# Decode attention on one core: K and V loaded in 2 KB runs with K four batches ahead, and the output projection turned round

## The chip, the cores and the metric

One core of one Trainium2 chip. The metric is device time in microseconds of the core, the median of several executions. A "span" is the length of the profiled execution, some 2 us shorter than the time reported for the same execution.

## The reference

One new token per sequence (32 sequences), 32 query heads on 8 K/V heads, attention over the last 512 of 2048 cached keys. Cut to what matters:

```python
B, Sq, D = 32, 1, 512
Hq, Hkv, Sk, Dh = 32, 8, 2048, 128
W = min(4096, max(256, Sk // 4))                     # 512 keys
q = (x @ wq) -> [B, Hq, 1, Dh]
k, v = k_cache[:, :, Sk - W:], v_cache[:, :, Sk - W:]  # each K/V head serves 4 query heads
p = softmax(q k^T / sqrt(Dh)); o = p v
return o -> [B, 1, Hq * Dh] @ wo
```

Everything is bf16. K and V of the window are 32 MiB each, wq and wo 4 MiB each: 75.5 MB are read for little arithmetic.

## The kernel before

Four sequences ("batches") make a block of 128 query rows; there are eight blocks. For each batch 1 MiB of K and 1 MiB of V come in, K is transposed on TensorE and evicted, and the scores of the block's 32 (batch, head) pairs accumulate in one PSUM tile through a masked q. Then come softmax, transposes of p, and PV.

```python
kpool = ... bufs=5;  vpool = ... bufs=7;  ktpool = ... bufs=6
# wo: four nc.scalar.dma_start, right after the q projection
def k_ap(b):                                          # v_ap(b) the same
    return k_cache[b, :, k0:Sk, :].rearrange("g (p c) d -> p g (c d)", c=NC)   # NC = 4: runs of 4*128*2 B = 1 KB
for j in range(NBLK):
    ...
    for bb in range(BB):
        nc.sync.dma_start(out=knat[:], in_=k_ap(b))
        nc.sync.dma_start(out=vt[:], in_=v_ap(b))
        # 32 transposes of 128x128 -> kps (PSUM); copies to kt on VectorE and ScalarE
    for bb, g:  nc.tensor.matmul(sc[:], lhsT=mask_flat[...], rhs=kt_tiles[bb][:, g, :], ...)
    # reduce_max, Exp -> p_sb, reciprocal, p_sb *= rs
    for c in range(NC):  nc.tensor.transpose(pT_ps[:, c, :], p_sb[:, c * P : (c + 1) * P], ident[:])
    nc.vector.tensor_copy(out=pT_sb[:], in_=pT_ps[:])
    for bb, g, c:  nc.tensor.matmul(oT[:, 4 columns], lhsT=v_tiles[bb][:, g, c * Dh : (c + 1) * Dh], rhs=pT_sb[...])
    # oT -> O_all
for h in range(Hq):
    nc.tensor.matmul(out_ps[:], lhsT=O_all[:, h, :], rhs=wo_sb[:, h, :], start=(h == 0), stop=(h == Hq - 1))
```

## Time and profile before

| | before |
|---|---|
| time, median before the prediction (3 runs) | 246.91 us (244.85 to 247.32) |
| span of the profiled execution | 242.8 us |
| DMA row | full from 6 to 218 us; 348 GB/s once wq is in |
| TensorE busy | 182.4 us, 75% |
| mean granted TensorE clock | 0.817 |
| last K landed at | 219.3 us |
| from there to the end | 23.5 us |

How to read it: first the rows of the page that cut the span into 40 slices, to see whether one resource is full from end to end; then the table of windows, for its rate in stages that differ; then the chain of waits in order of time, for what lies after the last load. The lines themselves are in the prediction.

### The profile page before, as it was taken

Reading aid. Unit: us, or ns where it says so; the run is one execution under the profiler, and the core shown is the slowest. Engines: PE = TensorE matmul, PEld = TensorE weight load, DVE = VectorE, ACT = ScalarE, POOL = GpSimd, SP = SyncE. Lnnn points to the kernel's source line nnn. Section 1 sums busy time; section 2 is a strip of 40 time slices with the busy share of each in tenths; the row PEclk is TensorE's granted clock in tenths of the full one; section 3 lists DMA queues with packets and bytes.
Section 4 is the critical chain, followed back from the end, with each engine's and each line's share of the span. In section 5 each row is a group of like instructions: output and inputs, shape, how many; then the busy total and the mean of one; then the engine's idle time right before and its main releaser. Section 6 shows DMA issues by size and latency. Waiting matters only on the chain.

```text
span 242.8 us, 5379 instructions
## 1 busy us (share of the span) xinstructions
PE 182.4 (75%) x2483; PEld 135.8 (56%) x2500; DVE 81.8 (34%) x146; ACT 50.0 (21%) x59; POOL 2.5 (1%) x7
## 2 busy tenths in 40 slices
PE   0327232988996869789969976899699969986694
PEld 0326232558754837486748744866496649654631
DVE  3023020235335315423553434136333453344201
ACT  0000130212132113301520422113402420232000
POOL 4000000000000000000000000000000000000000
PEclk9999675699599659965995899569956995699769
DMA  5999999999999999999999999999999999991000
GB/s 201 388 362 348 348 348 348 349 348 349 348 348 348 349 351 348 349 348 349 348 349 348 349 349 348 349 350 351 348 349 350 348 350 348 341 337 58 3 0 5
DMA packets 72950, 75.90 MB, mean 313 GB/s; under 512 B 1184, under 2 KB 70880, under 8 KB 72928
## 3 DMA queue, kind: packets, MB, share of 16 engines
q1 hardware_dynamic: 68768, 71.37, 91.6%
q10 hardware_dynamic: 4160, 4.19, 5.4%
q8 instruction: 19, 0.31, 0.5%
q14 instruction: 3, 0.02, 0.0%
HBM read 75.53 MB, written 0.03 MB: 311 GB/s over the span
## 4 chain that ended last, share of the span: by engine, by line
DMA 45%; PE 36%; SPq 8%; DVE 5%; ACT 2%; issue 2%; ACTq 0%
DMA knat<-in_k_cache_dram 36%; PE kps L158 13%; PE oT L213 11%; PE sc L175 7%; SPq L151 5%; DMA wq_t<-in_wq_dram 5%; DMA wo_sb<-in_wo_dram 5%; PE out_ps L232 4%; SPq L149 3%; ACT p_sb L190 2%; DVE mx L185 2%; PE pT_ps L204 1%; DVE p_sb L200 1%; SPq L88 1%; DVE rs L199 0%
## 5 line engine op out<-in xcount | busy, mean ns | idle before, releaser
L158 PE MATMUL kps<-ident,knat 128*128 128x128 bf16 x1024 | 79.7, 247 | 25.6 <-DMA knat<-in_k_cache_dram 23.4
L158 PEld LDWEIGHTS <-knat 128*128 128x128 bf16 x1024 | 73.6, 113 | 35.3 <-DMA knat<-in_k_cache_dram 28.3
L164 DVE COPY kt<-kps 128x1024 bf16<-128x1024 bf16 x86 | 57.5, 689 | 89.5 <-PE kps L158 89.1
L166 ACT COPY kt<-kps 128x1024 bf16<-128x1024 bf16 x42 | 42.5, 1013 | 127.0 <-PE kps L158 127.0
L175 PE MATMUL sc<-kt,maskB 128*128 128x512 bf16 x120 | 34.9, 427 | 1.1 <-issue 0.9
L175 PE MATMUL sc<-kt,maskA 128*128 128x512 bf16 x119 | 33.3, 415 | 1.0 <-issue 0.7
L213 PEld LDWEIGHTS <-vt 128*128 128x128 bf16 x1024 | 28.5, 103 | 1.0 <-issue 0.6
L213 PE MATMUL oT<-pT_sb,vt 128*128 128x4 bf16 x1024 | 28.4, 166 | 0.5 <-DVE pT_sb L206 0.5
L175 PEld LDWEIGHTS <-maskA 128*128 128x128 bf16 x128 | 13.3, 109 | 14.5 <-issue 5.1
L175 PEld LDWEIGHTS <-maskB 128*128 128x128 bf16 x128 | 13.3, 110 | 14.5 <-issue 6.0
L204 PE MATMUL pT_ps<-ident,p_sb 128*128 128x128 bf16 x32 | 3.8, 254 | 17.0 <-DVE p_sb L200 16.8
L221 DVE CAST O_all<-oT 128x128 bf16<-128x128 f32 x8 | 5.8, 719 | 26.0 <-PE oT L213 26.0
L204 PEld LDWEIGHTS <-p_sb 128*128 128x128 bf16 x32 | 2.2, 110 | 20.6 <-DVE p_sb L200 20.6
L96 PE MATMUL qT_ps<-xT_sb,wq_t 128*128 128x32 bf16 x128 | 4.1, 188 | 8.1 <-DMA wq_t<-in_wq_dram 8.1
L232 PE MATMUL out_ps<-wo_sb,O_all 128*32 128x512 bf16 x32 | 8.9, 447 | 0.8 <-DVE O_all L221 0.8
L190 ACT ACTIVATE p_sb<-sc,nbias 128x512 bf16<-128x512 f32 x8 | 5.5, 688 | 18.6 <-DVE nbias L187 18.6
L185 DVE TENSOR_REDUCE mx<-sc 128x1 f32<-128x512 f32 x8 | 5.5, 692 | 9.9 <-PE sc L175 9.9
L96 PEld LDWEIGHTS <-wq_t 128*128 128x128 bf16 x128 | 3.7, 104 | 8.5 <-DMA wq_t<-in_wq_dram 8.5
L166 ACT ACT_TABLE_LOAD x1 | 1.3, 1283 | 29.2 <-DMA knat<-in_k_cache_dram 29.2
L232 PEld LDWEIGHTS <-O_all 128*32 128x32 bf16 x32 | 3.5, 111 | 5.8 <-issue 2.4
L103 DVE CAST qT_sb<-qT_ps 128x1024 bf16<-128x1024 f32 x1 | 1.2, 1225 | 12.0 <-PE qT_ps L96 12.0
L206 DVE COPY pT_sb<-pT_ps 128x512 bf16<-128x512 bf16 x8 | 3.4, 424 | 4.1 <-PE pT_ps L204 4.1
(18 smaller groups left out, 14.9 us busy)
## 6 DMA issues: line engine op xcount, KB each, us to landing
knat<-in_k_cache_dram SPq DMA_DIRECT2D x32, 1024.0 KB, 12.0
vt<-in_v_cache_dram SPq DMA_DIRECT2D x32, 1024.0 KB, 11.9
wq_t<-in_wq_dram SPq DMA_DIRECT2D x4, 1024.0 KB, 8.5
wo_sb<-in_wo_dram ACTq DMA_DIRECT2D x4, 1024.0 KB, 19.3
x_sb<-in_x_dram SPq DMA_DIRECT2D x1, 32.0 KB, 1.6
out_dram<-out_sb SPq DMA_DIRECT2D x1, 32.0 KB, 1.5
```

The lines of the kernel that those rows point to most:

```text
L96: nc.tensor.matmul(qT_ps[:, h, :], lhsT=wq_t[:, cc, hl * Dh : (hl + 1) * Dh], rhs=xT_sb[:, cc, :], start=(cc == 0), stop=(cc == CC - 1),)
L149: nc.sync.dma_start(out=knat[:], in_=k_ap(b))
L151: nc.sync.dma_start(out=vt[:], in_=v_ap(b))
L158: nc.tensor.transpose(kps[:, gi, c, :], knat[:, g, c * Dh : (c + 1) * Dh], ident[:])
L164: nc.vector.tensor_copy(out=dst, in_=src)
L166: nc.scalar.copy(out=dst, in_=src)
L175: nc.tensor.matmul(sc[:], lhsT=mask_flat[:, P * t : P * t + P], rhs=kt_tiles[bb][:, g, :], start=(t == 0), stop=(t == NT - 1),)
L185: nc.vector.reduce_max(out=mx[:], in_=sc[:], axis=AX.X)
L190: nc.scalar.activation(out=p_sb[:], in_=sc[:], func=ACT.Exp, bias=nbias[:], scale=scale, accum_out=ssum[:],)
L204: nc.tensor.transpose(pT_ps[:, c, :], p_sb[:, c * P : (c + 1) * P], ident[:])
L213: nc.tensor.matmul(oT[:, rep * t : rep * t + rep], lhsT=v_tiles[bb][:, g, c * Dh : (c + 1) * Dh], rhs=pT_sb[:, c, rep * t : rep * t + rep] ...
L232: nc.tensor.matmul(out_ps[:], lhsT=O_all[:, h, :], rhs=wo_sb[:, h, :], start=(h == 0), stop=(h == Hq - 1),)
```

## The change

Its intent: longer runs for the transfers that bound the kernel, nothing left to do after the last load but a little PV, and a shorter projection.

* Two K/V heads share a tile: each head gives 64 rows of 8 keys (2 KB runs), one head to the even partitions, the other to the odd ones. The scores read each head's keys with a step of two elements. p is written twice over (each key for both heads of a pair), transposed in eight pieces, and masked so that each query head keeps its own partitions; PV then takes a pair of heads at once, eight columns for four.
* The scores of a batch stand directly behind its transposes. K is issued four batches (one block) ahead of V; wo comes in four pieces during blocks 2 to 5 from SyncE.
* The projection holds wo still and streams O: 128 matmuls of 32 columns for 32 of 512, then four transposes.

```diff
+    KLEAD = BB
+    kpool = ... bufs=7      # was 5;  vpool 7 as before;  ktpool bufs=3, was 6
+        return k_cache[b, :, k0:Sk, :].rearrange("(gp g2) (p c) d -> g2 p gp (c d)", g2=2, c=2 * NC)
+        for g2 in range(2):
+            nc.sync.dma_start(out=knat[g2::2, :, :], in_=k_ap(b)[g2])      # V the same
+    for bpre in range(min(KLEAD, B)):
+        issue_k(bpre)
...
+            if b + KLEAD < B:
+                issue_k(b + KLEAD)
+            issue_v(b)
+            if bb == 0 and 2 <= j < 2 + N_WO_CHUNKS:
+                issue_wo(j - 2)
...
-                    rhs=kt_tiles[bb][:, g, :],
+                    rhs=kt[:, g // 2, :].rearrange("p (k g2) -> p g2 k", g2=2)[:, g % 2, :],
...
-        nc.vector.tensor_scalar_mul(out=p_sb[:], in0=p_sb[:], scalar1=rs[:])
+        nc.vector.tensor_scalar_mul(
+            out=p_d[:], in0=p_sb[:].unsqueeze(2).to_broadcast([P, NC * P, 2]), scalar1=rs[:]
+        )
...                                       # eight transposes of p_d for four of p_sb
-        nc.vector.tensor_copy(out=pT_sb[:], in_=pT_ps[:])
+        nc.vector.tensor_tensor(out=pT_sb[:], in0=pT_ps[:], in1=own[:] (broadcast), op=mult)
...
-                        rhs=pT_sb[:, c, rep * t : rep * t + rep],
+                        rhs=pT_sb[:, c, 2 * rep * t : 2 * rep * (t + 1)],
...
-            out_ps[:], lhsT=O_all[:, h, :], rhs=wo_sb[:, h, :],
+                outT_ps[:, mc, :], lhsT=wo_sb[:, h, mc * P : (mc + 1) * P], rhs=O_all[:, h, :],
```

More of the change, by code (lines that the diff above doesn't have):

```diff
@@ L48 @@
     M = wo.shape[1]
-    assert M <= 512
+    assert M % P == 0 and M <= 512
+    MC = M // P
+    KLEAD = BB
     x2 = x.rearrange("b q d -> (b q) d")
@@ L58 @@
     x_sb = consts.tile([B, D], BF16, name="x_sb")
-    nc.sync.dma_start(out=x_sb[:], in_=x2[:, :])
     qT_sb = consts.tile([P, Hq, B], BF16, name="qT_sb")
@@ L68 @@
     masks = [maskA, maskB]
+    par = consts.tile([P, 2], FP32, name="par")
+    nc.vector.reduce_sum(out=par[:], in_=ident[:].rearrange("q (p g) -> q g p", g=2), axis=AX.X)
+    own = consts.tile([P, P], BF16, name="own")
+    nc.vector.tensor_copy(
+        out=own[:].rearrange("q (a g i) -> q a g i", g=2, i=rep),
+        in_=par[:].unsqueeze(1).unsqueeze(3).to_broadcast([P, P // (2 * rep), 2, rep]),
+    )
+    kpool = ctx.enter_context(tc.tile_pool(name="kpool", bufs=7))
+    vpool = ctx.enter_context(tc.tile_pool(name="vpool", bufs=7))
@@ L70 @@
+    ktpool = ctx.enter_context(tc.tile_pool(name="ktpool", bufs=3))
     N_WQ_CHUNKS = 4
     WQ_CHUNK_H = Hq // N_WQ_CHUNKS
-    with tc.tile_pool(name="psq", bufs=1, space=bass.MemoryType.PSUM) as psq, tc.tile_pool(
-        name="wqp", bufs=N_WQ_CHUNKS, side="right"
-    ) as wqp:
-        xT_ps = psq.tile([P, CC, B], BF16, name="xT_ps")
-        for cc in range(CC):
-            nc.tensor.transpose(
-                xT_ps[:, cc, :], x_sb[:, cc * P : (cc + 1) * P], ident[0:B, 0:B]
-            )
-        nc.vector.tensor_copy(out=xT_sb[:], in_=xT_ps[:])
-        qT_ps = psq.tile([P, Hq, B], FP32, name="qT_ps")
-        wq_r = wq.rearrange("(cc c) n -> c cc n", c=P)
-        wq_tiles = []
-        for ci in range(N_WQ_CHUNKS):
-            h0 = ci * WQ_CHUNK_H
-            wq_t = wqp.tile([P, CC, WQ_CHUNK_H * Dh], BF16, name="wq_t")
-            nc.sync.dma_start(out=wq_t[:], in_=wq_r[:, :, h0 * Dh : (h0 + WQ_CHUNK_H) * Dh])
-            wq_tiles.append(wq_t)
-        for ci in range(N_WQ_CHUNKS):
-            h0 = ci * WQ_CHUNK_H
-            wq_t = wq_tiles[ci]
-            for hl in range(WQ_CHUNK_H):
-                h = h0 + hl
-                for cc in range(CC):
-                    nc.tensor.matmul(
-                        qT_ps[:, h, :],
-                        lhsT=wq_t[:, cc, hl * Dh : (hl + 1) * Dh],
-                        rhs=xT_sb[:, cc, :],
-                        start=(cc == 0),
-                        stop=(cc == CC - 1),
-                    )
-        nc.vector.tensor_copy(out=qT_sb[:], in_=qT_ps[:])
@@ L105, with k_ap, v_ap @@
-    kpool = ctx.enter_context(tc.tile_pool(name="kpool", bufs=5))
-    vpool = ctx.enter_context(tc.tile_pool(name="vpool", bufs=7))
-    ktpool = ctx.enter_context(tc.tile_pool(name="ktpool", bufs=6))
+    wq_r = wq.rearrange("(cc c) n -> c cc n", c=P)
+    def k_ap(b):
+        return k_cache[b, :, k0:Sk, :].rearrange("(gp g2) (p c) d -> g2 p gp (c d)", g2=2, c=2 * NC)
+    def v_ap(b):
+        return v_cache[b, :, k0:Sk, :].rearrange("(gp g2) (p c) d -> g2 p gp (c d)", g2=2, c=2 * NC)
+    knat_tiles = {}
@@ new lines, with issue_k, issue_v @@
+    v_tiles = {}
+    def issue_k(b):
+        knat = kpool.tile([P, Hkv // 2, 2 * NC * Dh], BF16, name="knat")
+        for g2 in range(2):
+            nc.sync.dma_start(out=knat[g2::2, :, :], in_=k_ap(b)[g2])
+        knat_tiles[b] = knat
+    def issue_v(b):
+        vt = vpool.tile([P, Hkv // 2, 2 * NC * Dh], BF16, name="vt")
+        for g2 in range(2):
+            nc.sync.dma_start(out=vt[g2::2, :, :], in_=v_ap(b)[g2])
+        v_tiles[b] = vt
+    nc.sync.dma_start(out=x_sb[:], in_=x2[:, :])
@@ new lines @@
+    pctx = ExitStack()
+    psq = pctx.enter_context(tc.tile_pool(name="psq", bufs=1, space=bass.MemoryType.PSUM))
+    wqp = pctx.enter_context(tc.tile_pool(name="wqp", bufs=N_WQ_CHUNKS, side="right"))
+    wq_tiles = []
+    for ci in range(N_WQ_CHUNKS):
+        h0 = ci * WQ_CHUNK_H
+        wq_t = wqp.tile([P, CC, WQ_CHUNK_H * Dh], BF16, name="wq_t")
+        nc.sync.dma_start(out=wq_t[:], in_=wq_r[:, :, h0 * Dh : (h0 + WQ_CHUNK_H) * Dh])
+        wq_tiles.append(wq_t)
+    for bpre in range(min(KLEAD, B)):
+        issue_k(bpre)
@@ new lines @@
+    xT_ps = psq.tile([P, CC, B], BF16, name="xT_ps")
+    for cc in range(CC):
+        nc.tensor.transpose(xT_ps[:, cc, :], x_sb[:, cc * P : (cc + 1) * P], ident[0:B, 0:B])
+    nc.vector.tensor_copy(out=xT_sb[:], in_=xT_ps[:])
+    qT_ps = psq.tile([P, Hq, B], FP32, name="qT_ps")
+    for ci in range(N_WQ_CHUNKS):
+        h0 = ci * WQ_CHUNK_H
+        wq_t = wq_tiles[ci]
+        for hl in range(WQ_CHUNK_H):
+            h = h0 + hl
+            for cc in range(CC):
+                nc.tensor.matmul(
+                    qT_ps[:, h, :],
+                    lhsT=wq_t[:, cc, hl * Dh : (hl + 1) * Dh],
+                    rhs=xT_sb[:, cc, :],
+                    start=(cc == 0),
+                    stop=(cc == CC - 1),
+                )
@@ L108 @@
+    nc.vector.tensor_copy(out=qT_sb[:], in_=qT_ps[:])
+    pctx.close()
     wop = ctx.enter_context(tc.tile_pool(name="wop", bufs=1, side="right"))
@@ L112, with issue_wo @@
     hw_ = Hq // N_WO_CHUNKS
-    for i in range(N_WO_CHUNKS):
-        nc.scalar.dma_start(
+    def issue_wo(i):
+        nc.sync.dma_start(
             out=wo_sb[:, i * hw_ : (i + 1) * hw_, :],
@@ L125 @@
     ops_pool = mctx.enter_context(tc.tile_pool(name="ops", bufs=1, space=bass.MemoryType.PSUM))
-    def k_ap(b):
-        return k_cache[b, :, k0:Sk, :].rearrange("g (p c) d -> p g (c d)", c=NC)
-    def v_ap(b):
-        return v_cache[b, :, k0:Sk, :].rearrange("g (p c) d -> p g (c d)", c=NC)
     kt_evac_ctr = 0
@@ L142 @@
         )
-        kt_tiles = []
-        v_tiles = []
+        sc = scps_pool.tile([P, NC * P], FP32, name="sc")
+        t = 0
         for bb in range(BB):
             b = j * BB + bb
-            knat = kpool.tile([P, Hkv, NC * Dh], BF16, name="knat")
-            nc.sync.dma_start(out=knat[:], in_=k_ap(b))
-            vt = vpool.tile([P, Hkv, NC * Dh], BF16, name="vt")
-            nc.sync.dma_start(out=vt[:], in_=v_ap(b))
-            kt = ktpool.tile([P, Hkv, NC * P], BF16, name="kt")
-            for gp in range(Hkv // 2):
-                kps = ktps_pool.tile([P, 2, NC, P], BF16, name="kps")
-                for gi in range(2):
-                    g = gp * 2 + gi
-                    for c in range(NC):
-                        nc.tensor.transpose(
-                            kps[:, gi, c, :], knat[:, g, c * Dh : (c + 1) * Dh], ident[:]
-                        )
-                dst = kt[:, gp * 2 : gp * 2 + 2, :]
-                src = kps[:].rearrange("p a c q -> p a (c q)")
+            if b + KLEAD < B:
[3 more added lines that the diff above has]
+                issue_wo(j - 2)
+            knat = knat_tiles.pop(b)
+            kt = ktpool.tile([P, Hkv // 2, 2 * NC * P], BF16, name="kt")
+            for gp in range(Hkv // 2):
+                kps = ktps_pool.tile([P, 2 * NC, P], BF16, name="kps")
+                for c in range(2 * NC):
+                    nc.tensor.transpose(kps[:, c, :], knat[:, gp, c * Dh : (c + 1) * Dh], ident[:])
+                dst = kt[:, gp, :]
+                src = kps[:].rearrange("p c q -> p (c q)")
                 if kt_evac_ctr % 3 != 2:
@@ L167 @@
                 kt_evac_ctr += 1
-            kt_tiles.append(kt)
-            v_tiles.append(vt)
-        sc = scps_pool.tile([P, NC * P], FP32, name="sc")
-        t = 0
-        for bb in range(BB):
             for g in range(Hkv):
@@ L199 @@
         nc.vector.reciprocal(out=rs[:], in_=ssum[:])
-        nc.vector.tensor_scalar_mul(out=p_sb[:], in0=p_sb[:], scalar1=rs[:])
-        pT_ps = ptps_pool.tile([P, NC, P], BF16, name="pT_ps")
-        for c in range(NC):
-            nc.tensor.transpose(pT_ps[:, c, :], p_sb[:, c * P : (c + 1) * P], ident[:])
-        pT_sb = ppool.tile([P, NC, P], BF16, name="pT_sb")
-        nc.vector.tensor_copy(out=pT_sb[:], in_=pT_ps[:])
+        p_d = ppool.tile([P, NC * P, 2], BF16, name="p_d")
+        nc.vector.tensor_scalar_mul(
+            out=p_d[:], in0=p_sb[:].unsqueeze(2).to_broadcast([P, NC * P, 2]), scalar1=rs[:]
+        )
+        pT_ps = ptps_pool.tile([P, 2 * NC, P], BF16, name="pT_ps")
+        for c in range(2 * NC):
+            nc.tensor.transpose(
+                pT_ps[:, c, :], p_d[:, c * (P // 2) : (c + 1) * (P // 2), :].rearrange("r p g -> r (p g)"), ident[:]
+            )
+        pT_sb = ppool.tile([P, 2 * NC, P], BF16, name="pT_sb")
+        nc.vector.tensor_tensor(
+            out=pT_sb[:], in0=pT_ps[:], in1=own[:].unsqueeze(1).to_broadcast([P, 2 * NC, P]), op=mybir.AluOpType.mult
+        )
         oT = ops_pool.tile([P, P], FP32, name="oT")
@@ L210 @@
         for bb in range(BB):
-            for g in range(Hkv):
-                for c in range(NC):
+            vt = v_tiles.pop(j * BB + bb)
+            for gp in range(Hkv // 2):
+                for c in range(2 * NC):
                     nc.tensor.matmul(
-                        oT[:, rep * t : rep * t + rep],
-                        lhsT=v_tiles[bb][:, g, c * Dh : (c + 1) * Dh],
-                        rhs=pT_sb[:, c, rep * t : rep * t + rep],
+                        oT[:, 2 * rep * t : 2 * rep * (t + 1)],
+                        lhsT=vt[:, gp, c * Dh : (c + 1) * Dh],
+                        rhs=pT_sb[:, c, 2 * rep * t : 2 * rep * (t + 1)],
                         start=(c == 0),
-                        stop=(c == NC - 1),
+                        stop=(c == 2 * NC - 1),
                     )
@@ L229 @@
     ops2 = ctx.enter_context(tc.tile_pool(name="ops2", bufs=1, space=bass.MemoryType.PSUM))
-    out_ps = ops2.tile([B, M], FP32, name="out_ps")
-    for h in range(Hq):
-        nc.tensor.matmul(
-            out_ps[:],
-            lhsT=O_all[:, h, :],
-            rhs=wo_sb[:, h, :],
-            start=(h == 0),
-            stop=(h == Hq - 1),
-        )
+    outT_ps = ops2.tile([P, MC, B], FP32, name="outT_ps")
+    for mc in range(MC):
+        for h in range(Hq):
+            nc.tensor.matmul(
+                outT_ps[:, mc, :],
+                lhsT=wo_sb[:, h, mc * P : (mc + 1) * P],
+                rhs=O_all[:, h, :],
+                start=(h == 0),
+                stop=(h == Hq - 1),
+            )
+    outT_sb = outp.tile([P, MC, B], BF16, name="outT_sb")
+    nc.vector.tensor_copy(out=outT_sb[:], in_=outT_ps[:])
+    out_tps = ops2.tile([B, M], BF16, name="out_tps")
+    for mc in range(MC):
+        nc.tensor.transpose(out_tps[:, mc * P : (mc + 1) * P], outT_sb[:, mc, :], ident[:])
     out_sb = outp.tile([B, M], BF16, name="out_sb")
-    nc.vector.tensor_copy(out=out_sb[:], in_=out_ps[:])
+    nc.vector.tensor_copy(out=out_sb[:], in_=out_tps[:])
     nc.sync.dma_start(out=out2[:, :], in_=out_sb[:])
```

## The prediction

> **What bounds the kernel now.** I read the page's slices first, because they show whether one resource is full from end to end.
>
> ```profile
> PE   0327232988996869789969976899699969986694
> PEclk9999675699599659965995899569956995699769
> DMA  5999999999999999999999999999999999991000
> GB/s 201 388 362 348 348 348 348 349 348 349 348 348 348 349 351 348 349 348 349 348 349 348 349 349 348 349 350 351 348 349 350 348 350 348 341 337 58 3 0 5
> DMA packets 72950, 75.90 MB, mean 313 GB/s; under 512 B 1184, under 2 KB 70880, under 8 KB 72928
> ```
>
> The DMA row is full from slice 1 to slice 35 and the rate is flat at 348 GB/s: for nine tenths of the span the transfers set the pace, and TensorE (PE row) has gaps. Nearly every packet is under 2 KB; K, V and wo come as runs of 512 elements, 1 KB. Only slices 1 and 2 are faster. Those carry wq, whose runs are 1024 elements, 2 KB. So next I read the table of windows, short ones in the wq stage and a long one in the steady stage (last three columns: granted clock, DMA share, GB/s).
>
> ```profile
> 10.00:11.00 1.00, 0.16 (x6) 0.05 (x2) 0.00 (x0) 0.00 (x0) 0.00 (x0) 1.00 1.05 389
> 11.00:12.00 1.00, 0.17 (x6) 0.17 (x7) 0.00 (x0) 0.00 (x0) 0.00 (x0) 1.00 1.05 389
> 125.00:155.00 30.00, 22.72 (x343) 17.70 (x343) 11.78 (x24) 7.52 (x10) 0.00 (x0) 0.84 1.10 348
> ```
>
> 2 KB packets run at about 389 GB/s, 1 KB packets at 348. Then the chain that ended last, in order of time: one block's boundary in the middle, and the end.
>
> ```profile
> 98.40 1.79 PE kps L158 x32
> 100.19 1.74 PE sc L175 x8
> 101.93 0.02 issue
> 101.95 0.69 DVE mx L185
> ...
> 104.33 0.40 PE pT_ps L204 x4
> 104.73 1.04 PE kps L158 x10
> 105.77 3.39 PE oT L213 x128
> ...
> 206.30 13.01 DMA knat<-in_k_cache_dram
> ...
> 219.35 1.96 PE kps L158 x32
> 221.31 1.74 PE sc L175 x8
> ...
> 226.32 3.49 PE oT L213 x128
> ```
>
> The reader sees two things. The last K lands at 219.3, and only then come its transposes, its scores, the softmax chain, all of the last block's PV, the output projection and the store: 23.5 us of the 242.8 lie after the last load. And per batch TensorE needs 1.79 + 1.74 us at full clock, far less than the 6.0 us that 2 MiB take at 348 GB/s.
>
> **What the Trainium skill says.** (1) "SBUF — State Buffer", section "Door 1: The DMA port swizzle": DMA bandwidth depends on how many of 16 SBUF ports the partitions of a transfer reach; partitions 0 to 63 reach only 8 of them and were measured at 196 GB/s against 328 for all 128. The new loads take 64 partitions, but every second one, and by the page's table those touch all 16 ports. The same section says that strided reads stay at full speed with at least two hits per 16-byte line; the new scores read keys with a step of 4 bytes, four hits. No load of the kernel before writes every second partition and no matmul of it reads with a step, so the trace neither agrees nor disagrees. (2) "DMA: Bandwidth & Descriptors", section "Why a DMA increments its semaphore by 16 and not by 1": the largest divisor up to 16 of the slowest dimension gives the number of DMA engines, so 64 rows still use 16. Which rows go to which engine it does not say for 64 rows; that is my largest doubt. (3) "VectorE: DVE Perf Modes", section "The perf-mode tier table": tensor_tensor with a PSUM operand runs at the 1x rate, a copy from PSUM at up to 2x. The trace agrees for copies: 1024 bf16 elements from PSUM took 689 ns, 1024 f32 ones 1225. (4) "TensorE: Matmul & The Clock Gate", section "HAM oscillation": an idle gap of about 3.4 us halves the clock. Here the clock falls to 0.50 after each softmax gap although that is only some 2.5 us.
>
> ```profile
> 126.00:127.50 1.50, 0.00 (x0) 0.00 (x0) 0.65 (x4) 0.78 (x2) 0.00 (x0) 1.00 1.10 348
> 129.00:130.50 1.50, 1.50 (x48) 1.50 (x45) 0.69 (x1) 0.00 (x0) 0.00 (x0) 0.50 1.10 348
> 130.50:132.00 1.50, 1.50 (x63) 1.50 (x60) 0.00 (x0) 0.00 (x0) 0.00 (x0) 0.50 1.10 347
> ```
>
> **The change part by part.** *Loads.* K and V come in 2 KB runs, 64 half-tile issues of 0.5 MiB for K and as many for V, in place of 1 KB runs. If they reach wq's rate, 1 MiB takes 1.0486/0.387 = 2.71 us, which is also the spacing at which the four wq pieces released TensorE (9.12, 11.83, 14.55). It was 1.0486/0.348 = 3.01. For 64 MiB of K and V that is 19 us less; wo keeps 1 KB runs. Total: wq done at 14.6, then 68 pieces (32 K, 32 V, 4 wo) at 2.71: loads end at 14.6 + 184 = 199 us, plus about 1 for wo, in place of 219.
>
> *Order.* K runs four batches ahead, so the last four pieces are V. After the last load only that V's share of PV would remain, not 23.5 us of chain, provided that TensorE has kept up. Counting pieces in issue order: block j's last V is piece 8j + 12 plus the wo pieces before it: block 5 at 14.6 + 56 x 2.71 = 166, block 6 at 188, block 7 at 199.
>
> *TensorE per block.* Transposes and scores 4 x (1.79 + 1.74) = 14.1 us; PV 3.4 (same 128 matmuls, each 26.5 ns, 8 columns for 4); p transposes 8 for 4, so 0.8. The softmax gap (101.93 to 104.33, 2.4 us) grows: the doubled, normalised p has 1024 elements with a step of 0 inside, so I take the 1x duration of 1024 elements, 1.2 us, for the 0.35 of now: gap 3.3. The mask multiply takes 0.7 to 1.2 for 0.42, half hidden by hoisted transposes: 0.7. Sum 22.3 us at full clock. The clock's fall to half covers some 6.8 us per block; PV in it kept its 3.4 us, the other half of it loses some 2 us: 24.3. Against that the loads' period is 8 x 2.71 = 21.7, or 24.4 in blocks 2 to 5, which carry a wo piece each. So TensorE, now well under the loads, comes level with them. Up to block 5 the loads still lead (166); after it I let TensorE set the end.
>
> *Projection.* 128 matmuls of 32 columns at PV's 26.5 ns are 3.4 us for 8.92; the extra copy (0.3), four transposes (0.3) and a final copy (0.5 for 0.68) take back about 0.4. All of this is on the path: net 5 us less.
>
> *Sum.* PV of block 5 starts at 166 to 167; two TensorE periods of 22.3 to 24.3 bring PV of block 7 to 211 to 215; PV 3.4, O_all 0.7, projection and copies 4.5, store and end 2.6 (as now, 240.2 to 242.8): span 222 to 227. The run lies 2 to 4 us above the span now (244.6 and the median 246.9 against 242.8). So about 226 us. Doubling the DVE work in the softmax costs nothing else: DVE was 34% busy.
>
> **The rivals.** *A: the half-partition loads collide.* If an engine gets four neighbouring rows, it writes to two ports in turn and shares both with another engine; in step, half the ports are idle at any time. For it: the page's 196 GB/s for 64 partitions; against it: even and odd partitions reach all ports, and nothing forces the engines into step. An estimate from the page's 27.2 GB/s per port: half overlapped gives about 280 GB/s, so 71.3 MB take 255 us and the time is 280; mild overlap at 340 gives loads to 224 and about 237 us, still faster since the tail is shorter. *B: TensorE binds throughout* because the strided score read is slower. If a score took twice its 216 ns, a block costs 6.9 us more, the period is about 30 us, and the time some 265. Against it: four hits per line. *C: TensorE is never the bound*, since transposes of the next block, whose K has landed long before, get hoisted into the softmax gap (ten already are, behind the p transposes). Then the end follows the loads more closely: PV of block 6 at 188, up to 7 us of block 7 done before it, time about 215. *D: the loads are faster but nothing else is*, because the buffers hold them back: seven V tiles are freed only by PV. Piece 20 (V of batch 7) needs PV of block 0, whose last V is piece 12: a slack of seven pieces, 19 us, so I count little on it.
>
> **Range and chances.** The main path gives 225 to 230, C 215, mild A 237, strong A or B 260 to 280. I weigh main path and C together at 0.6, mild A at 0.2, strong A or B at 0.2. That gives 226 with a range of 212 to 256; faster 0.76, same 0.07, slower 0.17. The margin for "same" (242 to 252) is thin, as the outcomes lie on either side of it.
>
> **What would show it right or wrong.** Right: GB/s in the steady slices near 385; the median spacing of landings 2.7 us per MiB; scores at full clock still 216 ns apart; PV still 3.4 us per block; no K wait of TensorE after block 1; a last stretch in which the DMA row is empty and TensorE works on. Wrong: GB/s under 340 with a full DMA row (A); scores 430 ns apart at clock 1.00 (B); the last PV waiting for V (C); gaps in the DMA row with SyncE waiting for PV (D).

## The result and the profile after

The changed kernel took 214.97 us (median of 12 runs, 214.82 to 215.28), the kernel before 245.54 us (15 runs, 244.68 to 247.32). The ratio is 0.8744 (95%: 0.8720 to 0.8767), so 12.6% faster. Ratios are computed as the mean time of one kernel's runs over that of the other's runs of the same rounds, so they are not quite the ratio of the medians quoted. Executions over 1.5% slower than the fastest of the same kernel are left out of the means. The prediction was 226 us with a range of 212 to 256.

The slices of the page of the changed kernel (tenths; the last but one row is the DMA rate):

```profile
PEclk9999999999999999999969969999799999979758
DMA  5999999999999999999999999999999999999500
GB/s 179 391 388 387 387 386 386 387 386 385 388 385 387 379 369 387 384 388 367 381 386 389 383 367 385 388 383 379 373 387 386 387 386 389 384 385 387 221 8 6
DMA packets 41207, 75.92 MB, mean 356 GB/s; under 512 B 2208, under 2 KB 6368, under 8 KB 41184
```

The rate is 383 to 389 GB/s wherever K and V move alone; the four dips, to 367 to 373 at the lowest, come where the four wo pieces with their 1 KB runs are issued (65.9, 90.5, 116.6 and 141.3 us). The row stays full to the end, and the granted clock, which fell in every block before, hardly falls (mean 0.944 for 0.817).

The chain that ended last, in order of time: start, length, what.

```profile
178.10 0.78 PE oT L243 x32
...
192.95 10.72 DMA vt<-in_v_cache_dram
...
203.72 1.03 PE oT L243 x32
204.74 0.02 issue
204.77 0.72 DVE O_all L251
205.49 0.04 issue
205.53 3.59 PE outT_ps L263 x128
```

The end now hangs on the last V, which is in at 203.7; one quarter of a block's PV (32 matmuls), the copy and the projection follow. TensorE is not far ahead here: it stands 0.40 us for the last V but one and 1.62 us for the last. From 203.7 to the end it is 9.6 us in place of 23.5. So the 29.5 us of span saved are 15.6 us of earlier loads (219.3 to 203.7) and 13.9 us of shorter tail.

TensorE's instructions in order of time, from one softmax to the next (in brackets the idle time before):

```profile
57.72 0.62 PE L229 MATMUL pT_ps<-ident,p_d 128*128 128x128 bf16 x8 [2.04 <-DVE p_d L224]
58.18 1.95 PE L187 MATMUL kps<-ident,knat 128*128 128x128 bf16 x32
59.97 1.97 PE L196 MATMUL sc<-kt,maskA 128*128 128x512 bf16 x7
61.78 0.94 PE L243 MATMUL oT<-pT_sb,vt 128*128 128x8 bf16 x32
...
77.94 0.62 PE L229 MATMUL pT_ps<-ident,p_d 128*128 128x128 bf16 x8 [2.04 <-DVE p_d L224]
```

PV (oT) comes in quarters of 32, one behind each batch of the *next* block's scores. In the kernel before it was a run of 128 between two blocks. Nothing in the source says so: the order was chosen when the source was compiled ("the scheduler", for short). A whole block takes 20.2 us (57.72 to 77.94); the periods before and after it are 20.0 and 20.6 us, with 0.23 us of waiting for K in the last of them. From the fourth on, periods are 23.6 to 26.1 us and contain waits for K, so the loads set them.

The last stretch in the table of windows (columns: PE, PEld, DVE, ACT, POOL busy, granted clock, DMA share, GB/s):

```profile
196.00:198.00 2.00, 0.50 (x8) 0.50 (x9) 1.19 (x3) 0.46 (x2) 0.00 (x0) 1.00 1.05 387
198.00:200.00 2.00, 1.22 (x47) 1.10 (x45) 0.69 (x1) 0.00 (x0) 0.00 (x0) 0.95 0.73 271
200.00:202.00 2.00, 1.60 (x59) 1.54 (x55) 0.00 (x0) 0.00 (x0) 0.00 (x0) 0.50 0.46 169
202.00:204.00 2.00, 0.38 (x14) 0.30 (x12) 0.00 (x0) 0.00 (x0) 0.00 (x0) 0.50 0.10 32
```

The loads do not stop at once. The full rate ends near 199, then the DMA share falls for 4 to 5 us. The records of single packets in the trace (the views do not print them) show 2 KB packets as quick as before, a median of 84 to 85 ns from 198 to 204 us for 88 ns earlier: so the rate falls because some of the engines are done before others. Why they are is not known.

### The profile page after: what moved, and what is told of

Same layout as the page of the kernel before. It is cut to its first block, busy times and chain, and to the rows that moved or that the text cites. A ratio compares the mean times of both kernels' runs of the same rounds, so it can differ in the third digit from the quotient of the medians.

```text
span 213.3 us, 5787 instructions
## 1 busy us (share of the span) xinstructions
PE 161.8 (76%) x2602; PEld 127.1 (60%) x2632; DVE 86.3 (40%) x149; ACT 50.0 (23%) x59; POOL 2.5 (1%) x7
## 4 chain that ended last, share of the span: by engine, by line
DMA 55%; PE 35%; DVE 3%; SPq 3%; issue 1%; ACT 1%
DMA knat<-in_k_cache_dram 44%; PE kps L187 15%; PE sc L196 13%; DMA vt<-in_v_cache_dram 11%; PE oT L243 3%; SPq L98 2%; PE outT_ps L263 2%; ACT p_sb L211 1%; DVE p_d L224 1%; SPq L115 1%; DVE mx L206 1%; PE pT_ps L229 1%; DVE O_all L251 0%; PE out_tps L274 0%; DVE rs L220 0%
## 5 line engine op out<-in xcount | busy, mean ns | idle before, releaser
L187 PE MATMUL kps<-ident,knat 128*128 128x128 bf16 x1024 | 68.2, 229 | 13.9 <-DMA knat<-in_k_cache_dram 13.9
L187 PEld LDWEIGHTS <-knat 128*128 128x128 bf16 x1024 | 63.5, 103 | 15.6 <-issue 14.6
L196 PE MATMUL sc<-kt,maskB 128*128 128x512 bf16 x112 | 31.4, 397 | 1.5 <-ACT kt L193 0.4
L243 PE MATMUL oT<-pT_sb,vt 128*128 128x8 bf16 x1024 | 30.2, 166 | 2.8 <-DMA vt<-in_v_cache_dram 2.0
L196 PE MATMUL sc<-kt,maskA 128*128 128x512 bf16 x114 | 31.0, 391 | 1.1 <-issue 0.2
L229 PE MATMUL pT_ps<-ident,p_d 128*128 128x128 bf16 x64 | 5.7, 241 | 16.7 <-DVE p_d L224 16.7
L229 PEld LDWEIGHTS <-p_d 128*128 128x128 bf16 x64 | 4.2, 107 | 17.5 <-DVE p_d L224 17.5
L233 DVE TENSOR_TENSOR pT_sb<-pT_ps,own 128x1024 bf16<-128x1024 bf16 x8 | 5.5, 692 | 6.5 <-PE pT_ps L229 6.5
L224 DVE TENSOR_SCALAR p_d<-p_sb,rs 128x1024 bf16<-128x1024 bf16 x8 | 6.0, 754 | 0.3
L139 DVE CAST qT_sb<-qT_ps 128x1024 bf16<-128x1024 f32 x1 | 1.2, 1225 | 11.8 <-PE qT_ps L132 11.8
L263 PE MATMUL outT_ps<-O_all,wo_sb 128*128 128x32 bf16 x128 | 3.6, 188 | 0.8 <-DVE O_all L251 0.8
```

What stands on the lines that cost most here:

```text
L187: nc.tensor.transpose(kps[:, c, :], knat[:, gp, c * Dh : (c + 1) * Dh], ident[:])
L196: nc.tensor.matmul(sc[:], lhsT=mask_flat[:, P * t : P * t + P], rhs=kt[:, g // 2, :].rearrange("p (k g2) -> p g2 k", g2=2)[:, g % 2, :], s ...
L224: nc.vector.tensor_scalar_mul(out=p_d[:], in0=p_sb[:].unsqueeze(2).to_broadcast([P, NC * P, 2]), scalar1=rs[:])
L229: nc.tensor.transpose(pT_ps[:, c, :], p_d[:, c * (P // 2) : (c + 1) * (P // 2), :].rearrange("r p g -> r (p g)"), ident[:])
L243: nc.tensor.matmul(oT[:, 2 * rep * t : 2 * rep * (t + 1)], lhsT=vt[:, gp, c * Dh : (c + 1) * Dh], rhs=pT_sb[:, c, 2 * rep * t : 2 * rep * ...
L263: nc.tensor.matmul(outT_ps[:, mc, :], lhsT=wo_sb[:, h, mc * P : (mc + 1) * P], rhs=O_all[:, h, :], start=(h == 0), stop=(h == Hq - 1),)
```

## The experiments

Twelve kernels, each timed in three rounds. All gave correct results except the eighth. The first six undo parts of the change, so that together with the changed kernel they show seven of the eight combinations of three parts: the 2 KB runs ("wide"), the lead of K, the new projection.

| kernel | wide | lead | projection | median us | ratio to before (95%) | span us |
|---|---|---|---|---|---|---|
| x1 | | | | 245.34 | 0.9983 (0.9953 to 1.0014) | 243.4 |
| x2 | | x | | 237.88 | 0.9682 (0.9652 to 0.9712) | 236.2 |
| x3 | x | | | 234.50 | 0.9530 (0.9481 to 0.9579) | 233.1 |
| x4 | x | x | | 220.47 | 0.8963 (0.8931 to 0.8995) | 218.5 |
| x5 | | x | x | 233.07 | 0.9464 (0.9416 to 0.9512) | 231.2 |
| x6 | x | | x | 230.48 | 0.9357 (0.9298 to 0.9416) | 227.7 |
| changed | x | x | x | 214.97 | 0.8744 (0.8720 to 0.8767) | 213.3 |

**x1: all three parts undone.** What is left is wo's later place on SyncE's queue, scores directly behind each batch, and the buffer counts.

```diff
-    KLEAD = BB
+    KLEAD = 0
-    ... "(gp g2) (p c) d -> g2 p gp (c d)", g2=2, c=2 * NC     (and all that goes with it)
+    ... "g (p c) d -> p g (c d)", c=NC
-    128 projection matmuls and four transposes
+    32 projection matmuls
```

> The changed kernel with its three main parts undone: 1 KB runs and the old PV, K not ahead, the old projection. What is left of the change: wo is loaded in four pieces during blocks 2 to 5 from SyncE, scores follow each batch, other buffer counts (7 K, 3 kt). Theory (time = end of the loads + what is left to do after them): same bytes at 348 GB/s and the whole chain after the last K, so 243 to 248 us, the same as before. Rival (part of the gain comes from wo's later place and the buffer counts): under 240 us.

Measured: 245.34 us, ratio 0.9983. The rest of the change is worth nothing by itself; the gain is in the three parts.

**x2: the lead alone** (x1 with `KLEAD = BB`).

> Of the three parts only the order: K four batches ahead of V, 1 KB runs, old projection. Theory: loads end at about 220 as before, after them 1 us of PV, 0.7 O_all, 8.9 projection, 0.7 copy, 2.6 store, together 14 in place of 23.5; span 234, time 236 us. Rival (the order matters only together with the wide runs, because TensorE is not done by then): 243 us or more.

Measured: 237.88 us, span 236.2. In its chain the last V releases PV at 222.1, and 14 us follow, as expected; the loads end 2 us later than I had put them.

**x3: the wide runs alone** (x1 with the 2 KB layout).

> Of the three parts only the 2 KB runs on 64 interleaved partitions with the doubled p: K is not ahead, old projection. Theory: loads end at 203 to 204, and the whole chain comes after them (2.0 transposes, 1.7 scores, 4.5 softmax to masked p, up to 3.4 PV, 0.7, 8.9, 0.7, 2.6 = 24.5), so span 228, time 230 us. Rival (without the lead TensorE with its longer softmax cannot keep up and holds buffers back): 235 us or more with gaps in the DMA row.

Measured: 234.50 us, 4.5 over the theory. The DMA row is full at 387 GB/s and ends near 202, with no gaps, so the rival's "holds buffers back" is not seen either; but three more batches of transposes and scores still stand after that. TensorE was behind by most of a block.

**x4: the changed kernel with the old projection.**

```diff
-                outT_ps[:, mc, :], lhsT=wo_sb[:, h, mc * P : (mc + 1) * P], rhs=O_all[:, h, :], ...
+        nc.tensor.matmul(out_ps[:], lhsT=O_all[:, h, :], rhs=wo_sb[:, h, :], ...)
```

> The changed kernel with the old projection (32 matmuls of 512 columns). Theory: all of the projection's saving is on the path at the end: 5 us more than the changed kernel, 220 us. Rival (the clock is at half in the last stretch, so the old projection of 8.9 us stays 8.9 but the new one is faster at full clock only): difference under 3 us.

Measured: 220.47 us; the spans differ by 5.2 us (218.5 against 213.3). The projection's saving is all on the path.

**x5: the changed kernel with 1 KB runs.**

> The changed kernel with 1 KB runs on all 128 partitions and the old PV; lead and new projection stay. Theory: loads at 348 GB/s end at about 220, tail as in the changed kernel less a little, 9.7 us: span 230, time 231 to 232 us. Rival (it is the interleaved half-partition transfers or their number, not the run length, that change the rate): DMA rate other than 348.

Measured: 233.07 us, steady rate 348 to 351 GB/s. This run alone does not rule the rival out, since it also goes back to 128 partitions and transfers of 1 MiB. The kernel before does: there wq moves in 2 KB runs in just that form, at 387 to 389 GB/s, and K and V in 1 KB runs at 348. So the run length sets the rate. The last V releases PV at 222.0, the rest takes 9.2 us. With the lead, the wide runs are worth 18 us of span (231.2 to 213.3); without it, 10.3 us (243.4 to 233.1 in x1 and x3).

**x6: the changed kernel without the lead** (`KLEAD = 0`).

> The changed kernel without the lead (K of a batch issued just before its V). Theory: loads still end at 203 to 204, and the last K's chain comes after them: 2.0 + 1.7 + 4.5 + up to 3.4 PV in place of 1 us of PV, so 8 to 11 us more: 223 to 226 us. Rival (PV interleaved with the scores hides it): under 219.

Measured: 230.48 us, 4.5 to 7.5 us more than expected, and the rival (under 219) fails too. TensorE's instructions in order of time show why:

```profile
166.21 0.62 PE L229 MATMUL pT_ps<-ident,p_d 128*128 128x128 bf16 x8 [2.82 <-DVE p_d L224]
167.61 3.48 PE L243 MATMUL oT<-pT_sb,vt 128*128 128x8 bf16 x128 [0.78 <-DVE pT_sb L233]
170.96 3.57 PE L187 MATMUL kps<-ident,knat 128*128 128x128 bf16 x32
...
190.44 0.62 PE L229 MATMUL pT_ps<-ident,p_d 128*128 128x128 bf16 x8 [2.77 <-DVE p_d L224]
```

Here PV is one run of 128, TensorE idles 2.82 us before the p transposes and 0.78 us behind them, and the next 32 transposes take 3.57 us in place of 1.79 to 1.95: the granted clock is 0.50 there. The period is 24.2 us, above the 21.7 us in which the loads bring a block. Its chain alternates between loads and TensorE up to 145 us and has no load in it after that. So without the lead TensorE binds the second half, at the very period (24.3) that the prediction had worked out for the changed kernel. This left two readings: does the lead help by its order of loads, or by the order of instructions which the scheduler picks when it is there? x9 and x10 tell them apart.

**x7: neighbouring partitions in place of every second one.** Same run length, same number of transfers and of compute instructions.

```diff
-            nc.sync.dma_start(out=knat[g2::2, :, :], in_=k_ap(b)[g2])
+            nc.sync.dma_start(out=knat[g2 * (P // 2) : (g2 + 1) * (P // 2), :, :], in_=k_ap(b)[g2])     # V the same
```

> The changed kernel with the two heads of a pair in the lower and the upper 64 partitions in place of every second one; the same 2 KB runs, number of transfers, matmuls and DVE operations. Port theory (the skill's SBUF page: 64 neighbouring partitions reach 8 of 16 ports): the rate falls to 196 to 218 GB/s, 64 MiB take 310 to 340 us, time 330 to 370 us. Rival (two such transfers in flight fill each other's ports, or ports do not matter): within 2% of 215 us.

Measured: 318.0 to 352.8 us over six runs; the two fast ones, 318.0 and 322.7, give the ratio 1.3007 (1.2856 to 1.3158). The profiled run was one of the slow ones (345.7 us); its rate:

```profile
DMA  7999999999999999999999999999999999999950
GB/s 274 312 210 211 213 213 214 215 212 214 211 216 210 215 232 216 221 217 220 238 215 220 221 223 227 221 223 228 235 211 243 254 260 253 251 249 244 240 127 8
```

The row is as full as before, but at 210 to 260 GB/s. The records of single packets say what is slow: a packet of 2 KB takes a median of 160 ns in this run (20 to 300 us), 88 ns in the changed kernel, and 85 to 88 ns in the wq stage of either, whose transfers cover all 128 partitions. The interleaving of the partitions, which looks like a detail of layout, decides between 0.87 and 1.30 of the time before. That the rate drifts up over the run, and the wide scatter of the times, are not explained, and no run shows by which mechanism a packet takes longer.

**x8: one wo piece loaded and used four times** (wrong result; the compute stays).

```diff
-            if bb == 0 and 2 <= j < 2 + N_WO_CHUNKS:
+            if bb == 0 and j == 2:
-                lhsT=wo_sb[:, h, mc * P : (mc + 1) * P],
+                lhsT=wo_sb[:, h % hw_, mc * P : (mc + 1) * P],
```

> Wrong result on purpose: only one of the four wo pieces is loaded and used four times; all compute stays. Theory (the loads set the end): 3 MiB less at about 348 to 387 GB/s, so 8 to 9 us less, 206 us. Rival (TensorE sets the end, as I predicted): no change, over 212 us.

Measured: 205.77 us, span 204.0 for 213.3: 9.3 us less for 3 MiB less. The loads set the end of the changed kernel; TensorE has slack.

**x9: the lead, but blocks kept apart on TensorE.** The first transpose of a block is tied behind the last PV matmul of the block before. TensorE's order of work in a block, run for run, is then that of x6.

```diff
+                    if last_pv is not None and bb == 0 and gp == 0 and c == 0:
+                        # ordering edge without a semaphore, same engine: this transpose after last_pv
```

> The changed kernel (K four batches ahead, as it is), but TensorE may start the next block's transposes only after the last PV matmul of this block: the order of instructions that the kernel without the lead has. Theory (the lead helps since it lets PV be woven between the scores; in blocks TensorE needs 24.1 us and binds): period of the p transposes 24 us in place of 20 to 21.7, and the whole PV and softmax of the last block after it: first p transposes at 38, seven periods later 206, then 0.6 + 0.8 + 3.5 + 0.7 + 3.6 + 1.3 + 2.6: span 219, time 221 us. Rival (only the place of the last loads counts): within 1% of the changed kernel, 215.

Measured: 233.37 us, ratio 0.9471. The period is 24.1 to 26.6 us from block 2 on, as the theory says, and all of the gain of the lead is gone. It is 12 us longer than I expected: the first period is 30.7 us (the p transposes start at 37.4 and 68.1), because TensorE now stands for 2.1 and 4.5 us until the third and fourth V are in, which the lead of K has pushed back, and runs at half clock after it; two later periods (26.1 and 26.6 us) have a wait as well. The rival fails.

```profile
42.79 1.01 PE L251 MATMUL oT<-pT_sb,vt 128*128 128x8 bf16 x32 [2.11 <-DMA vt<-in_v_cache_dram]
48.26 0.99 PE L251 MATMUL oT<-pT_sb,vt 128*128 128x8 bf16 x32 [4.46 <-DMA vt<-in_v_cache_dram]
68.08 0.62 PE L237 MATMUL pT_ps<-ident,p_d 128*128 128x128 bf16 x8 [2.82 <-DVE p_d L232]
69.48 3.56 PE L251 MATMUL oT<-pT_sb,vt 128*128 128x8 bf16 x128 [0.78 <-DVE pT_sb L241]
```

**x10: no lead, but PV woven in.** PV of the block before is issued batch by batch behind the scores.

```diff
-    KLEAD = BB
+    KLEAD = 0
+            if pv_before is not None:
+                pv_before(bb, last_sc)        # 32 PV matmuls of block j-1 behind the scores of (j, bb)
```

> The kernel without the lead, but PV of the block before woven between the scores of this block, batch by batch, as the changed kernel has it. Theory (weaving keeps TensorE's period under the loads' 21.7 us): TensorE is done with everything but the last K's chain when the loads end at 203: then 1.9 + 1.8 + 0.8 + 3.2 softmax + 0.6 + 0.7 + 3.5 PV + 0.7 + 3.6 + 1.3 + 2.6: span 222 to 224, time 225, some 5 less than without weaving. Rival (order of TensorE does not matter without the lead): 230 as before.

Measured: 224.12 us, ratio 0.9104: 6 us less than x6, as expected. TensorE's instructions in order of time show PV in quarters behind the scores, and TensorE waiting for K, so the loads lead again:

```profile
90.98 1.98 PE L197 MATMUL sc<-kt,maskB 128*128 128x512 bf16 x7
92.80 0.94 PE L251 MATMUL oT<-pT_sb,vt 128*128 128x8 bf16 x32
95.28 1.95 PE L188 MATMUL kps<-ident,knat 128*128 128x128 bf16 x32 [1.54 <-DMA knat<-in_k_cache_dram]
```

Together:

| ratio to before | PV in one run per block | PV woven between the scores |
|---|---|---|
| K not ahead | 0.9357 (x6) | 0.9104 (x10) |
| K four batches ahead | 0.9471 (x9) | 0.8744 (changed) |

The runs of this table stem from three chips, so only their ratios to the kernel before on the same chip are compared. With PV in one run the lead does not help (it costs 1%, in part by the late V of x9's first block). Woven, it brings 0.036, about 9 us. The lead pays in two ways: it takes the last K's chain out of the tail, and in its presence the scheduler weaves PV by itself.

**x11: K in 4 KB runs**, meant to be better than both kernels.

```diff
-        for g2 in range(2):
-            nc.sync.dma_start(out=knat[g2::2, :, :], in_=k_ap(b)[g2])
+        for g4 in range(4):
+            nc.sync.dma_start(out=knat[g4::4, :, :], in_=k_ap(b)[g4])       # 32 rows of 16 keys
-                    rhs=kt[:, g // 2, :].rearrange("p (k g2) -> p g2 k", g2=2)[:, g % 2, :],
+                    rhs=kt[:, g // 4, :].rearrange("p (k g4) -> p g4 k", g4=4)[:, g % 4, :],
```

> A version meant to be better: K alone in runs of 4 KB (32 rows for each of four heads, every fourth partition), the scores' keys read with a step of 4 elements, exp writes p in V's order; V as in the changed kernel. Packet theory (47.1 ns for 1 KB and 84.7 ns for 2 KB on each of 16 engines fit 9.5 ns + 36.7 ns per KB... so 4 KB at 410 GB/s): K's 33.6 MB take 81.8 us for 86.7: 5 us less, 210 us. Rivals: a step of 8 bytes slows the scores (over 1.85 us for 8, TensorE's period over 21.7): 215 or more; 32 partitions per transfer cost rate: DMA row full at less than 387.

(The "36.7 ns per KB" is a slip: the two packet times differ by 37.6 ns, and 9.5 + 4 x 37.6 = 159.9 ns is what gives 410 GB/s.)

Measured: 269.77 us, ratio 1.0952. The first rival holds. Six score matmuls at full clock (1.00 in the table of windows for both), first in the changed kernel's chain in order of time, then in this kernel's:

```profile
60.42 1.52 PE sc L196 x6
```

```profile
242.97 2.89 PE sc L197 x6
```

A step of four elements (8 bytes) makes a score matmul nearly twice as long; a step of two did not. TensorE's period becomes 30 us and binds from the start. From 40 to 67 us, before TensorE held the loads back, the page's rate is 393 to 397 GB/s, near the 398 that half 4 KB (410) and half 2 KB (387) would give by the packet theory. Earlier, from 24 to 30 us, it is only 302 to 342 with the DMA share still at 0.96, which is not explained. As a saving it could not show.

**x12: K and V in 4 KB runs.**

> K and V in runs of 4 KB, p four times over (16 p transposes per block, masked in two halves), one less buffer for kps and kt. Packet theory alone: loads end near 194, time 205 to 206. TensorE theory: period 20.2 + 0.5 (8 more transposes) + 0.8 to 1.6 (longer p copy and mask) = 21.5 to 22.3 us is over the loads' 20.5, so TensorE binds: 207 to 212, no better than K alone in 4 KB.

Measured: 288.73 us, ratio 1.1740. The period is 31 to 33 us. The same slow scores hide what the expectation was about; whether V in 4 KB runs would pay by itself stays open. The trace does settle the rate: from 15 to 21 us, where all packets are of 4 KB and TensorE holds nothing back yet, the table of windows has 407 and 414 GB/s, and the records of single packets a median of 160 ns. That is the packet theory's 410 and 159.9. A version with 4 KB runs of K whose transposes leave each head's keys side by side, so that the scores read with step one, was not run.

## Why the prediction was right or wrong

**Rate of the loads: right.** 387 GB/s for 2 KB runs was read off wq's stage and came out at 383 to 389. Rival A (colliding half-partition loads) did not happen with every second partition; x7 shows that a loss of this kind is real with neighbouring ones, and larger than my "half overlapped" estimate of 280 GB/s; whether it comes about as I described it is not shown.

**End of the loads: right up to 4 us.** I put it at 199 to 200. The full rate ends near 199, but the last V is in at 203.7, since the engines do not finish together. The term that was missing is this ragged end; the kernel before has it too (182 GB/s from 218 to 220).

**TensorE sets the end: wrong, this is the step that failed.** The prediction took 22.3 to 24.3 us per block and let TensorE bind after block 5. It measured 20.2 where no load held it up. The working was right for PV in one run per block: x6 shows 24.1 to 24.2, x9 24.1 at best. What did not hold is the assumption under it, that PV stays one run. With it woven, three terms of the sum go: the wait for the mask (0.78) is filled by transposes; the last quarter of PV (0.78) falls into the softmax gap, whose idle part is 2.04 us in place of 2.82; and the clock mostly stays up, so the 2 us for the half clock go too. Further terms were too large: p's doubling took 0.75 us where I took 1.2, the mask 0.69 where I allowed up to 1.2. Rival C ("TensorE is never the bound", about 215 us) is what happened, through weaving rather than through hoisted transposes alone. x8 shows it: 3 MiB less to load, 9.3 us less time. C's number is in part luck: it let most of block 7's work on TensorE and a whole PV follow 188 us, while in the trace the last V at 203.7 and a quarter of PV set the end. Of the signs, "the last PV waiting for V (C)" came true, and "no K wait of TensorE after block 1" did not: the chain hangs on K again and again from 72 us on. My 226 was 5% too high for this reason; x10's 224.12 is close to it by coincidence.

**Rival B (slow strided scores): right to reject for this change.** Eight scores took 1.81 us for 1.74. x11 shows how close it was: one more doubling of the step and it decides, with about the period (30 us) and the time (270 us) that B had worked out (30 and 265).

**Projection: right.** 3.59 us for the 128 matmuls (3.4 predicted), 0.30 + 0.60 + 0.41 for the copies and transposes, together 4.9 for 9.6 (8.92 + 0.68). x4: 5.2 us of span.

**Tail: right in kind, and it brought more than I credited.** Because TensorE kept up, only a quarter of PV was left after the last load, which I had named as the case "provided that TensorE has kept up" and then not believed.

**Rival D (V buffers hold the loads back): rightly counted little.** The DMA row has no gap in the changed kernel.

**Range and chances:** 215 lies near the low edge of the range, which reaches that far only because C was let in; the main path's own 225 to 230 was missed by 10 us, since I centred on the wrong bound of two that were level: 21.7 us per block of loads against 22.3 to 24.3 of TensorE.

## What to carry to other kernels

When two resources come out level in a prediction, find out which order the scheduler will give the one whose time depends on order; here it moved the period by 4 us per block, more than any instruction's price. A lead on loads is worth what the compute order lets it be worth: with PV in one run it cost 1%, with PV woven in it was worth 9 us. When a transfer covers only half of the partitions, choose which half by test: the same bytes, run lengths and counts differed by half in time.

## What the Trainium skill lacked or had wrong

* "SBUF — State Buffer", section "Door 1": it says that at least two hits per 16-byte line suffice for full speed. A moving operand with a step of 8 bytes (two hits) took 2.89 us for six matmuls of 512 columns, against 1.52 us with a step of 4 bytes (four hits).
* The same section gives the port map, but neither it nor "DMA: Bandwidth & Descriptors" says how the rows of a 64-row transfer from SyncE go to the engines, nor what every second partition costs. Measured: every second partition 387 GB/s, 64 neighbouring ones 210 to 260 GB/s (x7's profiled run, a slow one).
* "DMA: Bandwidth & Descriptors", section "Specifications", gives 512 B as the least transfer for line rate. Here runs of 1 KB gave 348 GB/s and of 2 KB 387 to 389 GB/s, in the kernel before with partitions and size of the transfer equal (K and V against wq); runs of 4 KB alone gave 407 to 414 GB/s (x12).
* "VectorE: DVE Perf Modes", section "The perf-mode tier table", has tensor_tensor with a PSUM operand at 1x. The mask multiply of 1024 bf16 elements from PSUM took 692 ns, as long as the 1024-element copy from PSUM (687 ns) which the table has at up to 2x; 1024 f32 elements from PSUM took 1225 ns.
* "TensorE: Matmul & The Clock Gate" speaks of idle gaps of about 3.4 us (section "HAM oscillation"); in the kernel before the clock fell to 0.50 after each of the seven softmax gaps of 2.4 us, in x6 after 2.82 us idle, 0.6 us of work and 0.78 us idle, in the changed kernel after two of the first seven gaps of 2.0 to 2.5 us. Its section "Part 4: PE-mode transpose" has transposes at some 275 ns without the high clock; here one by itself lasts a mean of 229 ns, but the clock does engage: 32 in a row took 1.79 us, 56 ns from start to start, at clock 1.00, and 3.57 us at 0.50.
